# Hash-bucket attention and FFN: queries and keys as scaled high and low float16 halves, hash projections in four column blocks, six kept heads

## The chip, the cores and the metric

The kernel runs on one core of one Trainium2 chip. The metric is device time in microseconds. A core has a matrix engine (TensorE, in the profile PE, with its weight loads as PEld), VectorE (DVE), ScalarE (ACT), GpSimd (POOL), and SyncE (SP), whose queue issues most transfers here. Each engine takes its instructions in the order in which they are written.

## What is computed

The first stage is attention in which a query sees only keys of its own hash bucket; the second is a feed-forward net (FFN) over all tokens. There are 4 batches, 8 heads, 768 positions, 64 numbers per head, 6 hash bits, and an inner FFN width of 2048.

```python
q_bits = (np.einsum('bhsd,dk->bhsk', q, proj) > 0)
k_bits = (np.einsum('bhsd,dk->bhsk', k, proj) > 0)
mask = q_bucket[:, :, :, None] == k_bucket[:, :, None, :]
scores = scale * np.matmul(q, k.transpose(0, 1, 3, 2))
scores = np.where(mask, scores, -1000000000.0)
attn = softmax(scores)                    # with 1e-9 added to the sum
x = (attn @ v), heads side by side        # 3072 x 512
h = x @ w_in
out = (0.5 * h * (1 + erf(h / sqrt(2)))) @ w_out
```

## The kernel before

**Passes.** Attention works head by head. The first batch goes in two passes, one over the first 256 queries and one over the other 512, so that FFN work exists early; the other three batches go in one pass each. A pass prepares the operands of each head (`head`, L608) and then does units of 128 queries against all 768 keys (`unit`, L702): 2 units per head in the first pass, 4 in the second, 6 later, 192 in all. Each pair of heads ends in the product with V (`values`, L822). When all eight heads of a pass are through, its chunks of 256 tokens go through the FFN (L1025 and L1097).

**A head's operands.** `head` loads q and k, transposed and stacked to 128 rows (q in the upper 64, k in the lower), rounds them to fp32r into the tile Aq (the high half), and makes four tiles out of it: Ak gets a copy of the rounded k (L659), Bq and Bk get the other copies (L657, L658) and the low halves, which are what the rounding left (L660, L661). Copies can run on ACT, DVE, POOL or as a transfer on SP's queue; low halves on DVE or POOL. Then q and k are projected on the hash directions, in two column ranges of 256 and 512, each with three fp32r matmuls (L673, L675, L678); ACT takes the sign of each range (L681); two more operations write the mask rows (L691, L695). These rows lower a score by 2^34 for each hash bit in which query and key differ, so that softmax drops all keys of other buckets.

**Which heads are made again.** There are five operand sets in the first pass, of which two live only there. Heads 5 to 7 are made with all query columns and kept for the second pass, which goes through the heads in reverse; the other five are made again, for 512 query columns. Later batches have two sets.

**A unit.** Four fp32r matmuls of 384 columns (L716, L717) make the scores in PSUM; DVE takes the row maximum (L720), checks it (L724) and scales it (L729); ACT does the exponential with its sum (L732); DVE inverts the sum (L742). In the first 40 units TensorE turns the result (L789); in the others it is split into float16 halves (L380 or L377, and L748) and a transfer turns it.

**The order.** Nothing runs in program order. Each operation is a step with a cost, a key, the steps it needs and the buffer ring that it takes; many have a choice of engines. `Plan.order` (L91) plays all steps through on its own clock and gives, whenever an engine is free, the ready step of lowest key to it. The keys come from the unit's number and the offsets in `PAR` (L33); FFN matmuls have keys from 1000 on, so that they take TensorE when no attention step is ready. What comes out is the fixed order of each engine's instructions.

## Time and profile before

The median of three runs is 938.91 us (937.64 to 939.74). The profiled execution has a span of 936.0 us from its first to its last instruction; no other time of that one execution is given, and the 2.9 us to the median are what lies around the span.

| view | PE | DVE | ACT | POOL |
|---|---|---|---|---|
| busy, us of 936.0 | 882.8 | 727.8 | 611.0 | 300.4 |
| busy, 0 to 250 us (100 + 150) | 207.1 | 224.5 | 185.9 | 127.3 |
| busy, 250 to 750 us | 493.3 | 451.7 | 372.1 | 172.2 |
| busy, 750 to 936 us | 182.4 | 51.6 | 53.0 | 0.9 |

A line of the groups reads: source line, engine, operation, what it writes <- what it reads, shapes, count | busy us in all, mean ns of one | idle us of the engine just before them, and what ended it. In a line of the timeline the first number is the start and the second the length in us; a bracket gives the idle time before it. In a line of the chain of waits the numbers are start and length of a piece of the chain that ended last. A line of the windows gives the stretch, its length, then the busy time of each engine asked for, with instruction counts, the granted clock of TensorE, the share of DMA and GB/s. PE's matmuls are pipelined, so that one starts long before the last has ended.

### The profile page before, as it was taken

The page shows a single profiled execution, that of the slowest core. Times are in us where ns is not written, and L with a number is a line of the kernel's source. Part 1 is how long each engine was busy: PE and PEld are TensorE (multiplying, and loading weights), DVE is VectorE, ACT ScalarE, POOL GpSimd, SP SyncE. Part 2 cuts the span into 40 slices and gives each one's busy share as a digit, 9 for nine tenths or more (in the row PEclk, how much of TensorE's full clock was granted, in tenths as well). Part 3 has the DMA queues.
Part 4 walks back from the last instruction along what each step waited for, and adds up shares of the span by engine and source line. Part 5 has one row for each costly group of instructions (what it writes and reads, how often), then busy time and mean ns, then how long its engine had stood idle before and what let it go on. Part 6 is the DMA issues. An engine that isn't in the chain of part 4 may idle for free.

```text
span 936.0 us, 17821 instructions
## 1 busy us (share of the span) xinstructions
PE 882.8 (94%) x6728; PEld 645.9 (69%) x6728; DVE 727.8 (78%) x1616; ACT 611.0 (65%) x976; POOL 300.4 (32%) x254
## 2 busy tenths in 40 slices
PE   4788999877999999999999999999999999999998
PEld 3666788756676766677767776766776767676764
DVE  7899989889989899988889999889889972212122
ACT  5676877979676886867876767866788752222221
POOL 3553654556433233533142423342533100000000
PEclk9889999999999999999999999999999999999999
DMA  9447255267777799877797989688885860000000
GB/s 261 147 151 212 71 152 146 65 173 151 161 136 167 144 189 184 171 143 151 145 176 143 201 153 203 125 167 170 150 158 106 151 106 24 1 23 23 1 23 23
DMA packets 300822, 122.81 MB, mean 131 GB/s; under 512 B 241344, under 2 KB 285504, under 8 KB 300736
## 3 DMA queue, kind: packets, MB, share of 16 engines
q1 hardware_dynamic: 300560, 121.67, 60.0%
q8 instruction: 53, 0.87, 0.4%
q14 instruction: 33, 0.27, 0.1%
q10 hardware_dynamic: 176, 0.00, 0.0%
HBM read 45.49 MB, written 6.29 MB: 55 GB/s over the span
## 4 chain that ended last, share of the span: by engine, by line
PE 60%; DVE 8%; DMA 3%; ACT 3%; issue 1%; POOL 0%; SPq 0%; POOLq 0%; ACTq 0%; DVEq 0%
PE hp L1025 22%; PE hp L1097 21%; PE hp L846 6%; PE s L716 5%; PE s L717 4%; DVE rows L720 2%; DVE hl L748 2%; DMA pt<-hl 1%; DMA pt<-wraw 1%; ACT p L732 1%; DVE wraw L748 1%; DVE g L1073 1%; PE hp L673 1%; PE hp L678 1%; PE hp L675 1%
## 5 line engine op out<-in xcount | busy, mean ns | idle before, releaser
L1025 PE MATMUL hp<-x,Win 128*128 128x256 f16 x2304 | 267.0, 273 | 1.2 <-DVE rows L724 1.2
L1097 PE MATMUL hp<-Wout,g 128*128 128x512 f16 x1152 | 261.6, 379 | 0.0
L1025 PEld LDWEIGHTS <-Win 128*128 128x128 f16 x2304 | 219.8, 98 | 41.8 <-issue 13.5
L1097 PEld LDWEIGHTS <-g 128*128 128x128 f16 x1152 | 108.7, 98 | 128.3 <-issue 9.2
L720 DVE TENSOR_REDUCE rows<-s 128x1 f32<-128x768 f32 x192 | 179.3, 949 | 14.1 <-PE s L717 13.4
L732 ACT ACTIVATE p<-s,rows 128x768 f32<-128x768 f32 x143 | 141.1, 987 | 42.5 <-DVE rows L729 27.3
L716 PE MATMUL s<-Ak,Aq 128*128 128x384 f32 x352 | 137.7, 391 | 12.6 <-ACT p L732 7.0
L1035 ACT ACTIVATE h<-hp,ffs 128x512 f32<-128x512 f32 x96 | 65.6, 683 | 119.8 <-PE hp L1025 117.1
L717 PE MATMUL s<-Bk,Bq 128*128 128x384 f32 x352 | 120.5, 342 | 0.0
L380 DVE TENSOR_SCALAR g<-h,ffs 128x512 f16<-128x512 f32 x39 | 21.0, 541 | 112.7 <-ACT h L1059 82.0
L716 PEld LDWEIGHTS s<-Ak,Aq 128*128 128x128 f32 x352 | 67.8, 193 | 34.6 <-ACT p L732 10.9
L846 PE MATMUL hp<-pt,vhl 128*64 128x256 f16 x1368 | 82.3, 274 | 0.8 <-DMA pt<-hl 0.8
L846 PEld LDWEIGHTS <-vhl 128*64 128x64 f16 x1368 | 71.7, 110 | 12.3 <-issue 11.9
L748 DVE SCALAR_TENSOR_TENSOR hl<-p,rows,hl 128x768 f16<-128x768 f32 x72 | 76.0, 1058 | 2.8 <-ACT hl L377 1.6
L1073 DVE SCALAR_TENSOR_TENSOR g<-h,ffs,g 128x512 f16<-128x512 f32 x96 | 76.0, 810 | 2.4
L789 PE MATMUL hp<-dr,p 128*128 128x128 f32 x480 | 67.0, 296 | 8.2 <-DVE pt L380 2.4
L789 PEld LDWEIGHTS hp<-dr,p 128*128 128x128 f32 x480 | 63.2, 208 | 13.5 <-POOL dr L380 3.2
L717 PEld LDWEIGHTS s<-Bk,Bq 128*128 128x128 f32 x352 | 68.1, 193 | 1.2
L732 ACT ACTIVATE wraw<-s,rows 128x768 f32<-128x768 f32 x49 | 48.3, 986 | 13.8 <-DVE rows L729 5.7
L681 ACT ACTIVATE sign<-hp,off 44x256 f32<-44x256 f32 (+1 forms) x74 | 41.5, 570 | 22.7 <-PE hp L678 22.0
L400 POOL TENSOR_TENSOR Bq<-raw,Aq 64x768 fp32r<-64x768 f32 (+1 forms) x23 | 40.9, 1776 | 23.4 <-ACT Aq L377 13.0
L380 POOL TENSOR_SCALAR hl<-p,rows 128x768 f16<-128x768 f32 x24 | 26.3, 1097 | 63.1 <-DMA pt<-hl 42.0
(154 smaller groups left out, 1256.4 us busy)
## 6 DMA issues: line engine op xcount, KB each, us to landing
raw<-qk SPq DMA_DIRECT2D x29, 384.0 KB, 3.5
vraw<-v SPq DMA_DIRECT2D x25, 384.0 KB, 4.2
wraw<-w_in SPq DMA_DIRECT2D x16, 512.0 KB, 4.4
wraw<-w_out SPq DMA_DIRECT2D x16, 512.0 KB, 4.8
out<-o SPq DMA_DIRECT2D x11, 512.0 KB, 2.9
Ak<-Aq SPq DMA_DIRECT2D x19, 192.0 KB, 3.3
rawe<-qk SPq DMA_DIRECT2D x8, 384.0 KB, 3.1
Bk<-Aq SPq DMA_DIRECT2D x16, 192.0 KB, 3.3
```

What stands on the lines that cost most here:

```text
L380: on.tensor_scalar(out=out, in0=in_, scalar1=scale, scalar2=bias, op0=ALU.mult, op1=ALU.add)
L716: nc.tensor.matmul(to, aq[:, qs], ak[:, n], start=True, stop=False)
L717: nc.tensor.matmul(to, bq[:, qs.start - q0 : qs.stop - q0], bk[:, n], start=False, stop=True)
L720: nc.vector.tensor_reduce(out=nm, in_=both(sp), axis=AX.XY, op=ALU.max, negate=True)
L732: nc.scalar.activation(out=buf(ex).rearrange("p (b k) -> p b k", b=2), in_=both(sp), func=AF.Exp, scale=sc, bias=nb, accum_out=ssum,)
L748: nc.vector.scalar_tensor_tensor(out=buf(hi)[:, 1], in0=buf(ex), scalar=r, in1=buf(hi)[:, 0], op0=ALU.mult, op1=ALU.subtract,)
L789: nc.tensor.matmul(buf(step[0])[:, (k - k0) * P : (k - k0 + 1) * P], buf(ex)[:, words(k)], buf(dg), start=True, stop=True,)
L846: nc.tensor.matmul(pv[j * D : (j + 1) * D], buf(vh)[:, tv, kt, j * D : (j + 1) * D], buf(holds[j][0])[:, tp * KT + kt, :nt], start=kt == 0 ...
L1025: nc.tensor.matmul(buf(pair[0])[:, j * ch[1] : (j + 1) * ch[1]], win_hl[:, f0 // WB1, tw, pr, f0 % WB1 : f0 % WB1 + P], x[:, tx, pr, : ch[1]],
L1035: nc.scalar.activation(out=bufs["h"][0][:, 2 * fp : 2 * fp + 2, :nt], in_=buf(pair[0])[:, : 2 * nt].rearrange("p (j k) -> p j k", j=2), fu ...
L1073: nc.vector.scalar_tensor_tensor(out=gt[:, 1, s2, :nt], in0=h[:, s2, :nt], scalar=sg, in1=gt[:, 0, s2, :nt], op0=ALU.mult, op1=ALU.subtract,)
L1097: nc.tensor.matmul(buf(banks[u]).rearrange("p (c f) -> p c f", c=NWB), gt[:, tg, f, u * P : (u + 1) * P], wout_hl[:, :, tw, ft], start=ft ...
```

## The change

- All four operand tiles are float16. So that float16 suffices, each head gets a scale: DVE takes the largest magnitude in each row of the loaded head, two one-column matmuls against blocks of ones (`twin`) sum these over q's and k's rows, and four one-column DVE operations make a power of two out of it (`head_scale`). The rounding multiplies by it; the low half is scaled input less high half, one operation on DVE or two on POOL. The unit's check multiplies by the inverse (`back`) instead of a constant.
- The hash directions are float16 halves too. Columns 0 to 383 and 384 to 767 of q and of k are projected as four blocks of 32 array columns, with two terms: eight matmuls of 384 columns. One ACT operation takes all signs, and four operations write mask rows, each 24 rows by 384 columns. The sign's offsets come in by eight small transfers on SP's queue (`set_up`).
- With half the bytes, eight sets fit in the first pass, six stay for the second (heads 0 to 5), which makes heads 6 and 7 again, and four serve later batches. The second pass goes in forward order. The first makes all heads with all query columns.
- There are two buffers each for loaded heads of later passes, of the first pass, and for output (`o`, also used in scaling the weights).
- All keys and engine offsets in `PAR` have new numbers, and some costs in the plan differ. FFN, softmax and the product with V compute as before.

```diff
 NEARLY = 2
-RAWE = 1
-KEEP = 3
+RAWE = 2
...
+OB = 2
...
-BIG = 2.0**34
+PAR = dict(
+    SU=-208.01, NM_DVE=-120.92, NM_ACT=-21.45, NM_Pool=27.77, NM_SP=-123.06, NL_DVE=-286.91, NL_Pool=-152.59,
...
+    EV_ACT=-157.8, EV_DVE=400.19, EV_Pool=-118.56, GH_ACT=204.98, GH_DVE=104.62, GH_Pool=-464.69, NS0=-62.77,
+    NS1=-38.83, NS2=-129.58,
+)
+FULL = 65504.0
+FAR = 2.0**30
...
-        "s": 2, "hp": 4, "p": 2, "hl": 2, "raw": 1, "rawe": RAWE, "sign": 1, "dr": 2, "pt": NTH + 1,
-        "x": NTH, "vraw": 1, "vhl": 2, "wraw": 3, "o": 1, "diag": 1, "h": 1,
+        "s": 2, "hp": 4, "p": 2, "hl": 2, "raw": 2, "rawe": RAWE, "sign": 1, "dr": 2, "pt": NTH + 1,
+        "x": NTH, "vraw": 1, "vhl": 2, "wraw": 3, "o": OB, "diag": 1, "h": 1,
     }
-    NSET = 2
+    NSET = 4
+    NKEEP = 6
...
-        "sign": ring(const, "sign", [2 * 32, S], F32, 1),
+        "sign": ring(const, "sign", [P, S // 2], F16, 1),
...
-        "raw": ring(const, "raw", [P, S], F32, 1),
+        "raw": ring(const, "raw", [P, S], F32, rings["raw"]),
...
-    sets = [
-        [const.tile([P, S], F32R, tag=f"{nm}{i}", name=f"{nm}{i}") for nm in ("Aq", "Ak", "Bq", "Bk")]
-        for i in range(NSET)
-    ]
+    names = ("Aq", "Ak", "Bq", "Bk")
+    sets = [[const.tile([P, S], F16, tag=f"{nm}{i}", name=f"{nm}{i}") for nm in names] for i in range(NSET)]
...
-    rest = const.tile([P, S], F32R, tag="rest", name="rest")
-    x_ops = [t[:, :S] for t in ring(const, "x", [P, NPAIR * TC], F32R, NTH, NTH)]
-    sets.append([x_ops[0], x_ops[1], rest, x_ops[2]])
+    rest = const.tile([P, 2, S], F16, tag="rest", name="rest")
+    x_ops = [t[:, : 2 * S].rearrange("p (k n) -> p k n", k=2) for t in ring(const, "x", [P, 2 * NPAIR * TC], F16, NTH, NTH)]
+    for a, c in ((x_ops[0], x_ops[1]), (x_ops[2], rest)):
+        sets.append([a[:, 0], a[:, 1], c[:, 0], c[:, 1]])
...
+    for i in range(NKEEP, NKEEP + NEARLY):
+        sets.append([early.tile([P, S], F16, tag=f"{nm}{i}", name=f"{nm}{i}") for nm in names])
...
-    hash_hi = const.tile([P, KR + HR], F32R, tag="hash_hi", name="hash_hi")
-    hash_lo = const.tile([P, HR], F32R, tag="hash_lo", name="hash_lo")
...
+    twin = const.tile([P, 2, P], BF16, tag="twin", name="twin")
+    hash16 = const.tile([P, 2, 32], F16, tag="hash16", name="hash16")
+    off16 = const.tile([P, 1], F32, tag="off16", name="off16")
+    tops = const.tile([P, B * H + 3], BF16, tag="tops", name="tops")
+    hs = const.tile([P, B * H + 3, 8], F32, tag="hs", name="hs")
...
-    cleared = {}
-        def clear(ak=ak, box=box):
-            on = nc.vector if box[0].engine == "DVE" else nc.gpsimd
-            on.memset(ak[D:].bitcast(F32), 0.0)
-
...
+    def set_up():
+
+        top, w = tops[:, :1], hs[:, 0]
+        n_tops[0] += 1
+
+        def sums():
+            on = nc.gpsimd
+            on.memset(twin, 0.0)
+            for n in range(2):
+                rr = slice(n * D, (n + 1) * D)
+                on.memset(twin[rr, 0, rr], 1.0)
+                on.memset(twin[rr, 1, (1 - n) * D : (2 - n) * D], 1.0)
+            on.memset(hash16, 0.0)
+
+        def offsets():
+            for n in range(4):
+                for m in range(2):
+                    r0 = n * 32 + m * 2 * NBIT
+                    nc.sync.dma_start(out=off16[r0 : r0 + 2 * NBIT], in_=offset[: 2 * NBIT])
+
+        def clear():
+            nc.vector.memset(off16, 0.0)
+
+        def largest():
+            nc.vector.tensor_reduce(
+                out=top, in_=praw[:, :NBIT], axis=AX.X, op=ALU.max, apply_absolute_value=True
+            )
+
+        key = PAR["SU"]
+        a = add("Pool", 1.4, sums, key, [])
+        z = add("DVE", 0.1, clear, key, [])
+        o = add("SP", 0.5, offsets, key, [z])
+        m = add("DVE", 0.1, largest, key, [])
+        sc = head_scale(top, w, key, [a, m], 1)
+
+        def wide(n):
+            return hash16[:, n, : 4 * NBIT].rearrange("p (m i) -> p m i", m=2)
+
+        def high():
+            for m in range(2):
+                nc.vector.tensor_scalar(
+                    out=wide(0)[:, m], in0=praw, scalar1=w[:, 4:5], scalar2=None, op0=ALU.mult
+                )
+
+        def low():
+            for m in range(2):
+                nc.vector.scalar_tensor_tensor(
+                    out=wide(1)[:, m], in0=praw, scalar=w[:, 4:5], in1=wide(0)[:, m],
+                    op0=ALU.mult, op1=ALU.subtract,
+                )
+
+        hi = add("DVE", 0.2, high, key, [sc])
+        return [add("DVE", 0.2, low, key, [hi]), o]
+
+    def head_scale(top, w, key, needs, n):
+        def total():
+            for k in range(n):
+                nc.tensor.matmul(buf(pm)[:, k : k + 1], twin[:, k], top, start=True, stop=True)
+
+        def exponent():
+            nc.vector.tensor_scalar(
+                out=w[:, :n].bitcast(I32), in0=buf(pm)[:, :n].bitcast(I32), scalar1=0x7F800000,
+                scalar2=None, op0=ALU.bitwise_and,
+            )
+
+        def inverse():
+            nc.vector.tensor_scalar(
+                out=w[:, 2 : 2 + n], in0=w[:, :n], scalar1=2.0 if n > 1 else 2.0**-100, scalar2=2.0**-12,
+                op0=ALU.max, op1=ALU.mult,
+            )
+
+        def scale():
+            nc.vector.reciprocal(out=w[:, 4:5], in_=w[:, 2:3])
+
+        def back():
+            nc.vector.tensor_scalar(
+                out=w[:, 5:6], in0=w[:, 2:3], scalar1=w[:, 3:4], scalar2=SCALE, op0=ALU.mult, op1=ALU.mult
+            )
+
+        pm = add("PE", 0.06 + 0.08 * n, total, key, needs, takes="hp")
+        e = add("DVE", 0.12, exponent, key, [pm])
+        free(pm, [e])
+        e = add("DVE", 0.07, inverse, key, [e])
+        if n > 1:
+            e = add("DVE", 0.07, back, key, [e])
+        return add("DVE", 0.07, scale, key, [e])
+
+    def head(b, h, i, key, clear, cl):
+
+        n = n_tops[0]
+        n_tops[0] += 1
+        top, w = tops[:, n : n + 1], hs[:, n]
+        sc = w[:, 4:5]
+        aq, ak, bq, bk = sets[i]
+        upper, lower = slice(0, D), slice(D, P)
+
+        def load():
+            nc.sync.dma_start(out=buf(raw), in_=qk[b, h])
+
+        def largest():
+            nc.vector.tensor_reduce(
+                out=top, in_=buf(raw), axis=AX.X, op=ALU.max, apply_absolute_value=True
+            )
+
+        def high():
+            affine(hi.engine, aq, buf(raw), sc)
+
+        def add_move(dst, src, rd, rs):
+            box = []
+
+            def move():
+                out, in_ = sets[i][dst][rd], sets[i][src][rs]
+                if box[0].engine == "SP":
+                    nc.sync.dma_start(out=out, in_=in_)
+                else:
+                    affine(box[0].engine, out, in_)
+
+            on = {
+                "DVE": (0.27, PAR["NM_DVE"]), "ACT": (0.75, PAR["NM_ACT"]), "Pool": (0.9, PAR["NM_Pool"]),
+                "SP": (0.45, PAR["NM_SP"]),
+            }
+            box.append(add(on, 0, move, key + PAR[f"DUP{cl}"], [hi], port=True))
+            return box[0]
+
+        def add_low(dst, rd, rs):
+            box = []
+
+            def low():
+                out, a = sets[i][dst][rd], aq[rs]
+                x = buf(raw)[rs]
+                if box[0].engine == "DVE":
+                    nc.vector.scalar_tensor_tensor(
+                        out=out, in0=x, scalar=sc[rs], in1=a, op0=ALU.mult, op1=ALU.subtract
+                    )
+                else:
+                    affine("Pool", x, x, sc[rs])
+                    subtract("Pool", out, x, a)
+
+            on = {"DVE": (0.94, PAR["NL_DVE"]), "Pool": (2.8, PAR["NL_Pool"])}
+            box.append(add(on, 0, low, key + PAR[f"LOW{cl}"], [hi], port=True))
+            return box[0]
+
+        raw = add("SP", 1.43, load, key - PAR["HQ"], takes="raw" if cl else "rawe")
+        mx = add("DVE", 0.87, largest, key + PAR[f"NS{cl}"], [raw])
+        sc_ = head_scale(top, w, key + PAR[f"NS{cl}"], [mx, set16[0]], 2)
+        hi = add(affine_on("RND", S, True), 0, high, key, [sc_, *clear], port=True)
+        m1 = add_move(2, 0, upper, upper)
+        m2 = add_move(3, 0, lower, lower)
+        m3 = add_move(1, 0, upper, lower)
+        lq = add_low(2, lower, upper)
+        lk = add_low(3, upper, lower)
+        free(raw, [lq, lk])
+
+        space = add("none", 0, lambda: None, key, [m1, m2, lq, lk], takes="sign")
+        HS = S // 2
+
+        def signs_of():
+            return buf(space)
+
+        def project():
+            for t in range(2):
+                for half in range(2):
+                    n = slice(half * HS, (half + 1) * HS)
+                    for k, x in enumerate((bq, bk)):
+                        r0 = half * 64 + k * 32
+                        nc.tensor.matmul(
+                            buf(pp)[r0 : r0 + 32, :HS], hash16[:, t], x[:, n], start=t == 0, stop=t == 1,
+                            tile_position=(0, r0),
+                        )
+
+        def sign():
+            nc.scalar.activation(out=signs_of(), in_=buf(pp)[:, :HS], func=AF.Sign, bias=off16)
+
+        pp = add("PE", 0.45, project, key + PAR[f"PRJ{cl}"], [space, *set16], takes="hp")
+        sg = add("ACT", 0.1 + 0.833e-3 * HS + 0.186, sign, key + PAR[f"PRJ{cl}"], [pp])
+        free(pp, [sg])
+        masks = []
+        rows = slice(D, D + 4 * NBIT)
+        for half in range(2):
+            for k, dst in enumerate((0, 1)):
+                box = []
+
+                def mask(half=half, k=k, dst=dst, box=box):
+                    r0 = half * 64 + k * 32
+                    affine(
+                        box[0].engine, sets[i][dst][rows, half * HS : (half + 1) * HS],
+                        signs_of()[r0 : r0 + 4 * NBIT], FULL / 2, FULL / 2 if k == 0 else -FULL / 2,
+                    )
+
+                on = {
+                    "DVE": (0.18, PAR["NK_DVE"]), "ACT": (0.42, PAR["NK_ACT"]), "Pool": (0.56, PAR["NK_Pool"])
+                }
+                needs = [sg, m2, m3] if k == 0 else [sg]
+                box.append(add(on, 0, mask, key + PAR[f"MSK{cl}"], needs, port=True))
+                masks += box
+        free(space, masks)
+        return [m3, *masks], w[:, 5:6]
...
-    def head(b, h, i, key, clear, qr, cl):
...
-    def unit(t, i, q0, qs, cl, whole, made, place):
-
-        aq, ak, bq, bk = sets[i]
+    def unit(t, i, qs, cl, whole, made, place, back):
+
...
         def scores():
+            aq, ak, bq, bk = sets[i]
+            kk = slice(0, D + 4 * NBIT)
             for half in range(2):
                 n = slice(half * S // 2, (half + 1) * S // 2)
                 to = both(sp)[:, half]
-                nc.tensor.matmul(to, aq[:, qs], ak[:, n], start=True, stop=False)
-                nc.tensor.matmul(to, bq[:, qs.start - q0 : qs.stop - q0], bk[:, n], start=False, stop=True)
+                nc.tensor.matmul(to, aq[kk, qs], ak[kk, n], start=True, stop=False)
+                nc.tensor.matmul(to, bq[:, qs], bk[:, n], start=False, stop=True)
...
-                out=sc, in0=nm, scalar1=BIG / 2, scalar2=SCALE, op0=ALU.is_lt, op1=ALU.mult
+                out=sc, in0=nm, scalar1=FAR, scalar2=back, op0=ALU.is_lt, op1=ALU.mult,
...
-        sp = add("PE", 0.72, scores, t - PAR[f"QK{cl}"], made, takes="s")
+        sp = add("PE", 0.66, scores, t - PAR[f"QK{cl}"], made, takes="s")
...
+    set16 = set_up()
...
-        n_sets = NSET + 1 + NEARLY if n_pass == 0 else NSET + 1 if b == 0 else NSET
+        n_sets = NKEEP + NEARLY if n_pass == 0 else NKEEP if b == 0 else NSET
         n_head = (q1 - q0) // P
         cl = min(n_pass, 1) if b == 0 else 2
-        again = n_pass > 0 and b == 0
-        more = n_pass == 0 and len(FIRST) > 1
-        heads = list(range(2 * NPAIR))[:: -1 if again else 1]
+        heads = list(range(2 * NPAIR))
...
-                cols = (0, S) if more and pos >= len(heads) - KEEP else (q0, q1)
-                made = head(b, h, i, t - lead, last_use.get(i, cleared.get(i, [])), cols, cl)
-                owner[i] = (b, h, cols[0], made)
-            _, _, base, made = owner[i]
+                owner[i] = (b, h, *head(b, h, i, t - lead, last_use.get(i, []), cl))
+            made, back = owner[i][2:]
...
-            if i > NSET:
+            if i >= NKEEP:
...
-                plan.grow("x", k, spare_use)
+                plan.grow("x", k, last_use[NSET + (k - NTH) // 2])
```

126 lines of the change are left out of this document (19 added, 107 removed).

## The prediction

> **What bounds the kernel now.** I read the page's engine totals and its 40 slices first.
>
> ```profile
> PE 882.8 (94%) x6728; PEld 645.9 (69%) x6728; DVE 727.8 (78%) x1616; ACT 611.0 (65%) x976; POOL 300.4 (32%) x254
> PE   4788999877999999999999999999999999999998
> DVE  7899989889989899988889999889889972212122
> ```
>
> TensorE (PE) is full from the fifth slice on, except around slices 8 to 10. VectorE (DVE) is nearly full too, until slice 33, and then almost idle. An average would hide this, so I cut the span where the last product with V ends (778 us), and where the second pass of the first batch ends (about 225 us).
>
> ```profile
> 0.00:225.00 225.00, 184.83 (x1386) 151.07 (x1387) 200.88 (x459) 166.51 (x310) 111.13 (x99) 0.96 0.55 152
> 225.00:778.00 553.00, 543.60 (x4291) 392.38 (x4292) 492.22 (x1103) 404.26 (x621) 189.23 (x156) 1.00 0.79 156
> 778.00:936.00 158.00, 154.41 (x1056) 102.47 (x1052) 34.72 (x55) 40.21 (x46) 0.00 (x0) 1.00 0.04 14
> 0.00:100.00 100.00, 71.11 (x437) 57.68 (x437) 87.55 (x194) 65.12 (x124) 44.98 (x46) 0.91 0.63 186
> ```
>
> The columns after the length are PE, PEld, DVE, ACT, POOL busy. Before 225 us PE idles 40 us, 29 of them in the first 100: there is not yet an FFN to fill it. From 225 to 778 us it idles 9 us of 553, and after that it runs FFN alone. So from 100 us on a microsecond taken off PE is a microsecond off the end, as long as attention itself does not end later. How much later it may end, the chain of waits tells:
>
> ```profile
> 774.60 4.05 PE hp L846 x72
> ...
> 820.43 10.48 PE hp L1025 x96
> ...
> 862.12 10.48 PE hp L1025 x96
> ...
> 914.27 18.14 PE hp L1097 x84
> ```
>
> One FFN chunk of 256 tokens takes 862.12 - 820.43 = 41.7 us. The last batch has three, 125.1 us, and none can start before attention ends at 778.6. PE ends at 914.27 + 18.14 = 932.4, that is 153.8 us after, so 28.7 us of FFN of the batch before is still waiting there. The span cannot be below the attention's end + 125.1 + 3.6 (store).
>
> **The change part by part.** Spacing of matmuls, not their duration, is PE's price, as they are pipelined.
>
> ```profile
> 402.10 0.47 PE L673 MATMUL hp<-Aq,hash_lo 128*44 128x256 f32 x1
> ...
> 403.32 0.34 PE L716 MATMUL s<-Ak,Aq 128*128 128x384 f32 x1
> ...
> 403.85 0.34 PE L717 MATMUL s<-Bk,Bq 128*128 128x384 f32 x1
> ...
> 434.70 6.57 PE hp L1025 x60
> 389.13 5.20 PE hp L1097 x24
> ```
>
> *Scores.* A 384-column matmul of the old type starts every (403.85 - 403.32)/3 = 0.177 us (two lie between). In float16, 256 columns take 6.57/60 = 0.1095 us and 512 take 5.20/24 = 0.2167, so 384 lie at 0.163. Four per unit: 0.708 becomes 0.652 us. After 100 us the groups of the first of each pair are:
>
> ```profile
> L716 PE MATMUL s<-Ak,Aq 128*128 128x384 f32 x328 | 127.4, 389 | 8.6 <-ACT p L732 5.9 <-issue 1.4 <-ACT wraw L732 1.0
> L716 PE MATMUL s<-x,x 128*128 128x384 f32 x20 | 7.4, 370 | 0.0
> ```
>
> Two a unit, so (328 + 20)/2 = 174 units; the other 18 run where PE idles anyway. 174 x 0.056 = 9.7 us saved. Ends: 0 (the old spacing stays) and 174 x 4 x 0.015 = 10.4.
>
> *Projections.* Six matmuls now take 402.10 to 403.32, 1.22 us; the first is noted some 0.19 us early (it starts 0.03 us after the 512-column matmul ahead of it, which needs 0.22), so 1.03 us for a full head. A head of the second pass lacks one of 256 columns: 0.92. After the first pass, near 100 us, come 5 heads of pass two and 8 for each of three batches: 24 x 1.03 + 5 x 0.92 = 29.3 us. New are eight of 384 columns with 32-column weights, four beside each other. The trace has two beside each other, in the product with V:
>
> ```profile
> 640.73 0.34 PE L717 MATMUL s<-Bk,Bq 128*128 128x384 f32 x1
> 641.00 2.15 PE L846 MATMUL hp<-pt,vhl 128*64 128x256 f16 x36
> 643.09 0.43 PE L673 MATMUL hp<-Aq,hash_lo 128*44 128x512 f32 x1
> ```
>
> 36 in 2.09 us is 0.058 each, half of the 0.1095 of a full-width one: they do run side by side. Entering costs 0.27 - 0.18 = 0.09 us, leaving about as much (2.09 - 18 x 0.111). So a head costs 2 x 0.163 + 0.19 = 0.52 us, with 8 x 0.163 + 0.19 = 1.49 as the other end if the four do not overlap. I take 0.52, since the nearest row shows overlap. Two heads instead of five are made in pass two: 26 x 0.52 = 13.5. Saved: 15.8 us; other end, 26 x 1.49 = 38.7, a loss of 9.4.
>
> The Trainium skill (TensorE: Matmul & The Clock Gate, Part 3, "What overlaps and what doesn't") says that weight loads overlap matmuls in flight only where the row group differs, which speaks against column blocks that all use the full rows; the rows at 641.00 disagree for two blocks. The same part gives 2.38 times for three blocks of 32 columns; by that figure eight would cost an estimated 0.55 + 0.19 us, and the sum would be 6 us worse.
>
> *A scale per head.* Each head adds a maximum over 128x768 and four one-column operations on DVE, and two one-column matmuls between them. Their rows:
>
> ```profile
> L720 DVE TENSOR_REDUCE rows<-s 128x1 f32<-128x768 f32 x192 | 179.3, 949 | 14.1 <-PE s L717 13.4
> L724 DVE TENSOR_SCALAR rows<-rows 128x1 f32<-128x1 f32 x192 | 26.8, 146 | 0.9
> L729 DVE TENSOR_SCALAR rows<-rows 128x1 f32<-128x1 f32 x192 | 37.5, 208 | 1.8
> L742 DVE RECIPROCAL rows<-rows 128x1 f32<-128x1 f32 x192 | 31.0, 162 | 7.4 <-ACT rows L377 2.1
> L415 PE MATMUL hp<-diag,ones 128*128 128x128 bf16 x12 | 2.7, 226 | 7.0 <-ACT diag L377 3.9 <-DVE diag L380 1.5 <-POOL diag L380 0.8
> ```
>
> DVE: 0.95 + 0.15 + 0.15 + 0.21 + 0.16 = 1.62 us a head. PE: the nearest row, 128 columns, is 0.226 us for one with its latency, a floor for two is 2 x 0.03 us (the noted start-to-start above); I take 0.15: 26 x 0.15 = 3.9 us lost (ends 1.6 and 11.8). The 7.0 us that PE idled at 12 such matmuls, 0.58 us each, is a wait and not in this; see the rivals.
>
> *Rounding, moves, low halves, signs, masks.* The three moves and both low halves stay, as float16; two sign operations become one; two masks become four shorter ones. All lie on DVE, ACT, POOL and the DMA queue, hidden behind PE after 100 us. DVE's part in the long stretch is the one cover that may go:
>
> ```profile
> 250.00:778.00 528.00, 19.92 (x18) 1.00 0.79 156
> 250.00:778.00 528.00, 56.98 (x34) 1.00 0.79 156
> 350.00:400.00 50.00, 49.15 (x377) 34.11 (x377) 47.95 (x111) 36.45 (x56) 25.11 (x21) 1.00 0.83 173
> ```
>
> (The first two are what reads the raw heads: DVE 18 operations, POOL 34.) DVE then has 492.2 + 24 x 1.62 = 531 us, 96% of 553, the share that it reached at 350 us (47.95 of 50). ACT has 149 us free there and loses a sign operation and moves, so it can take over the "high" halves that DVE makes now. I take it as holding, narrowly: attention ends near 778 us. PE's work after 100 us falls by 9.7 + 15.8 - 3.9 = 21.6 us, less than the 28.7 us of FFN that are left over there, so PE does not run dry.
>
> *Start.* Two chains grow.
>
> ```profile
> 5.59 0.84 ACT L377 ACTIVATE Aq<-rawe 128x768 fp32r<-128x768 f32 x1 [1.87 <-DMA rawe<-qk]
> 11.47 0.69 PE L716 MATMUL s<-Ak,Aq 128*128 128x384 f32 x1 [1.68 <-POOL Ak L380]
> 1.34 1.06 ACTq L328 DMA_DIRECT2D off<-offset  x2
> ```
>
> Head 0 needs 5.9 us from landing to first score; the maximum, a matmul (0.23) and four small operations put about 1.8 us before it, and hops. Eight small transfers for the sign offsets go onto SP's queue, at 0.53 us each 4.2 us, ahead of loads of raw heads and V issued after them (nothing waits for the offsets until the first sign). Against it, moves are of 2 bytes, the zeroing of old operands goes, and pass two prepares two heads instead of five, at about 40 us of idle PE. Pass one, however, now prepares all 768 query columns of every head instead of 256 for five. I take +2 us, ends -12 and +10.
>
> *Six sets kept, two raw buffers, two output buffers, order and assignment by new numbers:* more lead for loads; nothing on PE.
>
> Sum: -9.7 - 15.8 + 3.9 + 2 = -19.6 us on the profiled span: 936.0 to 916.4. The median of the runs (938.91) is 2.9 above that span, for what lies around it: **919 us**.
>
> **The rivals.** The nearest row for a low half on DVE is that of P:
>
> ```profile
> L748 DVE SCALAR_TENSOR_TENSOR hl<-p,rows,hl 128x768 f16<-128x768 f32 x72 | 76.0, 1058 | 2.8 <-ACT hl L377 1.6 <-POOL hl L380 0.9
> ```
>
> (a) *DVE paces attention; slower.* If the low halves move from POOL to DVE (POOL must now do two operations for each), 48 x 1.06 us less the 19.9 that they take now is +31 on top of 531: 562 us, and at 96% the stretch takes 585 instead of 553. Attention ends at 225 + 585 = 810 us, + 128.7 = 939, + 2 from the start, + 2.9: 944. It decides as soon as attention ends after 788, and makes the kernel slower than before from 807. For it: DVE's 9s in the slices; against it: 149 us free on ACT and 364 on POOL.
>
> (b) *PE waits for the scale.* PE takes its work in a written order; a scale matmul that it reaches before DVE's maximum holds all scores and FFN behind it. At 0.58 us (L415) and 34 heads, 20 us: 939, no change. Against it: the maximum depends on a load alone, and four sets in place of two allow it early.
> (c) *Column blocks run one after another:* 25.2 us more, 944. The rule on weight loads quoted above would bring this; the V rows speak against it.
> (d) *The start shortens as well.* If fewer heads in pass two and the second output buffer take away the 14 us that PE idles between 100 and 225 (40.2 - 28.9 = 11.3, and as much again in the first 100 us at most): 919 - 2 - 14 = 903.
>
> **How the numbers follow.** Chances: forecast 0.48, (a) 0.11, (b) 0.14, (c) 0.04, (d) 0.20, else 0.03. A difference under 0.2% (1.9 us) can't be told from none here. Faster: forecast and (d) whole, 0.10 of (b) where the waits are shorter than 0.58 us, 0.04 of the rest: 0.82. Same: 0.05, mostly (b). Slower: 0.13. Range 898 to 939: from a (d) with 5 us more to (b) in full, which leaves out (a), (c) and a deeper (d), 0.2.
>
> **What would show it.** Scores spaced 0.163 us apart; eight projection matmuls within 0.55 us; PE's total near 860; FFN after attention's last V product still over 125 us with attention ending at or before 786 us. Wrong would be: idle before the scale matmuls of over 10 us in sum, eight projection matmuls over 1 us, or attention ending after 800 us with PE idle before it.

## The result

The changed kernel takes 931.16 us (median of 8 runs, 928.18 to 935.01) where the kernel before took 938.21 in the same comparison: a ratio of 0.9923, 95% interval 0.9903 to 0.9942. A second comparison, among the experiments below, gave 929.14 us and a ratio of 0.9871 (0.9843 to 0.9898). So it is faster by about 1% (0.8 to 1.3%); the forecast of 919 us meant 2%. One execution of one kernel below (u1) took 1781.57 us, nearly twice as long as the others, and is left out of its median. The profiled execution took 928.35 us with a span of 926.4.

The page of the changed kernel, its engine totals and the slices of PE and DVE:

```profile
PE 857.1 (93%) x6857; PEld 576.7 (62%) x6857; DVE 734.4 (79%) x1734; ACT 607.8 (66%) x990; POOL 347.1 (37%) x323
PE   1578899996999999999999999999999999999998
DVE  6888999999989999999999999899889961212122
```

PE's total fell from 882.8 to 857.1, near the 860 of the forecast. But the span fell by only 9.6: PE's idle time grew from 53.2 to 69.3 us. To see where, I cut both spans at two row maxima that DVE takes: the 49th, the first of the second batch (called unit 48 below, counted from 0), and the last (unit 191). Before, they start at 220.3 and 755.0 us, after at 223.9 and 743.5. First the windows before (length, then PE, PEld, DVE, ACT, POOL busy, clock, DMA share, GB/s):

```profile
0.00:220.30 220.30, 183.18 (x1358) 149.84 (x1358) 197.10 (x449) 161.85 (x306) 106.64 (x96) 0.96 0.54 152
220.30:755.00 534.70, 522.25 (x4127) 379.48 (x4128) 483.76 (x1091) 399.44 (x612) 193.23 (x159) 1.00 0.80 159
755.00:936.00 181.00, 177.41 (x1245) 116.61 (x1243) 46.97 (x80) 49.69 (x59) 0.49 (x1) 1.00 0.10 25
```

and the same windows after:

```profile
0.00:223.90 223.90, 171.22 (x1364) 122.55 (x1365) 203.48 (x518) 169.61 (x329) 115.84 (x111) 0.93 0.54 153
223.90:743.50 519.60, 506.81 (x4232) 335.62 (x4231) 483.37 (x1138) 387.83 (x602) 230.03 (x212) 1.00 0.79 153
743.50:926.40 182.90, 179.03 (x1264) 118.50 (x1262) 47.59 (x81) 50.40 (x60) 1.25 (x2) 1.00 0.10 26
```

In the long stretch PE has 15.4 us less to do and the stretch is 15.1 us shorter: one for one. In the first 48 units PE has 12.0 us less to do, and yet they end 3.6 us later; PE's idle time there grew from 37.1 to 52.7 us. Behind the last row maximum 1.9 us more went by. That is the whole 9.6: -15.1 + 3.6 + 1.9.

One more cut, at the first row maximum of the second pass (unit 16, at 98.0 us before and 106.8 after), parts the two passes of the first batch. Before, then after:

```profile
0.00:98.00 98.00, 69.61 (x427) 56.49 (x428) 85.55 (x188) 64.44 (x122) 43.15 (x44) 0.91 0.63 188
98.00:220.30 122.30, 113.57 (x933) 93.34 (x932) 111.54 (x262) 97.42 (x185) 63.49 (x53) 1.00 0.47 123
0.00:106.80 106.80, 65.90 (x453) 45.57 (x454) 89.82 (x229) 69.20 (x126) 47.90 (x51) 0.90 0.59 177
106.80:223.90 117.10, 105.32 (x912) 76.97 (x911) 113.66 (x290) 100.40 (x204) 67.94 (x61) 0.96 0.50 131
```

The first pass ends 8.8 us later: PE has 3.7 us less to do in it, but idles 40.9 us in place of 28.4. The second pass takes 5.2 us less. Not all of the PE work missing there is saved, for the new order puts FFN work off. The first matmul of the FFN's first product (L1025 before, L1120 after) starts at 112.6 us before and at 153.3 after. The same windows for these lines alone, before and after (PE busy, count), in the second pass and behind the last row maximum:

```profile
98.00:220.30 122.30, 22.49 (x192) 1.00 0.47 123
106.80:223.90 117.10, 14.71 (x111) 0.96 0.50 131
755.00:936.00 181.00, 77.79 (x696) 1.00 0.10 25
743.50:926.40 182.90, 80.41 (x720) 1.00 0.10 26
```

In the second pass 81 of these matmuls are missing, 8.9 us at the 0.1095 us that one takes in the prediction. They are done later: 24 of them behind the last row maximum, which is most of the 1.9 us there. The granted clock of the second pass also fell, from 1.00 to 0.96; no run here shows what that costs.

The matmuls themselves, in the timeline after (start, length; the PEld line is the loading of the eight projections' weights):

```profile
211.37 0.33 PE L816 MATMUL s<-Ak,Aq 88*128 88x384 f16 x1
211.53 0.33 PE L817 MATMUL s<-Bk,Bq 128*128 128x384 f16 x1
211.79 0.12 PEld L602 LDWEIGHTS <-hash 128*32 128x32 f16 x8 [0.32 <-issue]
211.79 0.34 PE L602 MATMUL hp<-Bq,hash 128*32 128x384 f16 x1
...
211.80 0.34 PE L602 MATMUL hp<-Bk,hash 128*32 128x384 f16 x1
211.96 0.33 PE L602 MATMUL hp<-Bq,hash 128*32 128x384 f16 x1
...
353.72 0.34 PE L602 MATMUL hp<-Bq,hash 128*32 128x384 f16 x1
...
354.16 1.04 PE L1192 MATMUL hp<-Wout,g 128*128 128x512 f16 x4
...
403.67 0.33 PE L816 MATMUL s<-Ak,Aq 88*128 88x384 f16 x1
...
404.83 0.33 PE L817 MATMUL s<-Bk,Bq 128*128 128x384 f16 x1
```

Scores lie 0.165 us apart, as from 403.67 to 404.83 us with six between them (0.163 forecast). Four projections start together, four more 0.17 us later; from the first to the next instruction it is 0.44 us, and entering costs 0.26 - 0.165 = 0.09, so 0.53 us a head (0.52 forecast). And PE's waits (us in total, times, longest):

```profile
PE hp L494 <- DVE tops L537: 25.3, 6, 7.3
PE s L816 <- ACT p L832: 13.1, 18, 2.6
PE s L816 <- ACT wraw L832: 8.2, 12, 1.7
```

PE waited 25.3 us for a head's maximum in front of scale matmuls, which the forecast named as a sign of rival (b). All six of these waits lie before unit 48; behind it no scale matmul waits. The experiments show what this sign is worth.

### The profile page after: what moved, and what is told of

It is laid out like the page before. It is cut to its first block, busy times and chain, and to the rows that moved or that the text cites. A ratio compares the mean times of both kernels' runs of the same rounds, so it can differ in the third digit from the quotient of the medians.

```text
span 926.4 us, 18281 instructions
## 1 busy us (share of the span) xinstructions
PE 857.1 (93%) x6857; PEld 576.7 (62%) x6857; DVE 734.4 (79%) x1734; ACT 607.8 (66%) x990; POOL 347.1 (37%) x323
## 4 chain that ended last, share of the span: by engine, by line
PE 35%; DVE 23%; DMA 4%; issue 4%; ACT 3%; POOL 1%; SPq 0%; POOLq 0%; DVEq 0%; ACTq 0%
PE hp L1192 14%; PE hp L1120 14%; DVE rows L820 5%; DVE hl L848 4%; PE hp L946 3%; DMA pt<-hl 3%; DVE wraw L848 2%; DVE g L1168 2%; PE s L816 2%; PE s L817 2%; DMA pt<-wraw 1%; ACT p L832 1%; DVE rows L824 1%; DVE rows L829 1%; DVE rows L842 1%
## 5 line engine op out<-in xcount | busy, mean ns | idle before, releaser
L1120 PE MATMUL hp<-x,Win 128*128 128x256 f16 x2304 | 269.9, 274 | 0.2
L1120 PEld LDWEIGHTS <-Win 128*128 128x128 f16 x2304 | 223.8, 98 | 41.1 <-issue 5.1
L832 ACT ACTIVATE p<-s,rows 128x768 f32<-128x768 f32 x140 | 138.0, 986 | 45.3 <-DVE rows L829 23.7
L816 PE MATMUL s<-Ak,Aq 88*128 88x384 f16 x360 | 120.9, 336 | 22.8 <-ACT p L832 12.8
L817 PE MATMUL s<-Bk,Bq 128*128 128x384 f16 x360 | 121.1, 336 | 0.0
L386 DVE TENSOR_SCALAR g<-h,ffs 128x512 f16<-128x512 f32 x30 | 15.2, 508 | 107.5 <-ACT h L1154 76.1
L832 ACT ACTIVATE wraw<-s,rows 128x768 f32<-128x768 f32 x52 | 51.3, 987 | 25.5 <-DVE rows L829 15.7
L817 PEld LDWEIGHTS <-Bq 128*128 128x128 f16 x360 | 35.8, 100 | 50.7 <-issue 33.7
L386 POOL TENSOR_SCALAR hl<-p,rows 128x768 f16<-128x768 f32 x34 | 38.2, 1122 | 57.4 <-DMA pt<-hl 34.0
L816 PEld LDWEIGHTS <-Aq 88*128 88x128 f16 x360 | 36.0, 100 | 31.5 <-issue 9.7
L386 POOL TENSOR_SCALAR raw<-raw,hs 64x768 f32<-64x768 f32 x30 | 34.5, 1151 | 43.2 <-ACT Aq L383 35.2
L1154 ACT ACTIVATE h<-h 128x2048 f32<-128x2048 f32 x24 | 45.9, 1911 | 0.4
```

The lines of the kernel that those rows point to most:

```text
L386: on.tensor_scalar(out=out, in0=in_, scalar1=scale, scalar2=bias, op0=ALU.mult, op1=ALU.add)
L816: nc.tensor.matmul(to, aq[kk, qs], ak[kk, n], start=True, stop=False)
L817: nc.tensor.matmul(to, bq[:, qs], bk[:, n], start=False, stop=True)
L832: nc.scalar.activation(out=buf(ex).rearrange("p (b k) -> p b k", b=2), in_=both(sp), func=AF.Exp, scale=sc, bias=nb, accum_out=ssum,)
L1120: nc.tensor.matmul(buf(pair[0])[:, j * ch[1] : (j + 1) * ch[1]], win_hl[:, f0 // WB1, tw, pr, f0 % WB1 : f0 % WB1 + P], x[:, tx, pr, : ch[1]],
```

## The experiments

The forecast's theory is that PE sets the end from 100 us on and that measuring the heads (maximum, scale matmuls, small operations) costs 0.15 us of PE a head and a part of about 2 us at the start, the rest being hidden. Against it stand: measuring costs VectorE's time (A); it costs through the chain behind the maximum (B, and F for the matmuls in it); the late start is handed on (C) or not (D); in the first 48 units VectorE sets the pace and PE's time counts for nothing (G). All edits keep each engine's order except where they move steps; nothing is planned anew. Medians of the kernel before, beside which each ratio stands, were 938.3 us (e1 to e4), 938.0 (e5, e6, s1, q1), 939.2 (c1 to c3, p2), 940.0 (u1, u2, d1) and 941.1 (a2, e8, e9). As the changed kernel itself came out at 0.9923 and at 0.9871, 4.9 us apart, differences of under 5 us between groups are not settled. Gains are given against its 931.16 us where nothing else is said. Each trace is of one execution, which lies up to 6 us beside the median of its runs.

**Leaving the measuring out (e2, e3).**

```diff
+            on.memset(hs[:, 1:, 4:5], 256.0)
+            on.memset(hs[:, 1:, 5:6], 2.0**-19)
...
+        if not measured:          # e2: cl in (0, 1); e3: all heads
+            for step in [mx, *plan.steps[n0:]]:
+                step.emit = lambda: None
```

> The changed kernel with a fixed scale for the ten heads of the first batch: their maxima, scale matmuls and small operations are left out, everything else keeps its place (the part of the computation left out is the measuring of the scale). Theory A: 5 to 7 us earlier first scores (about 17 us), and 923 to 927 us. Rival B: 10 of 34 heads, so a third of what leaving it out in all heads gains.

> The same fixed scale for all 34 heads (measuring left out everywhere). Theory A: like e2 within 2 us, since in later batches the measuring is hidden behind TensorE. Rival B: 24 x 1.6 us of DVE time fewer in the long stretch, attention ends 10 to 30 us earlier than in e2, total 900 to 915.

Measured: 923.03 us (ratio 0.9842, 0.9826 to 0.9857) and 916.68 us (0.9773, 0.9755 to 0.9791). Measuring costs 14.5 us in all, 8.1 for the ten heads of the first batch and 6.4 for the other 24. The 6.4 are between two runs of one comparison; the other two figures rest on the 931.16. With the second comparison's ratio of 0.9871 it is 9.2 us in all (0.9871 - 0.9773, of 938 us), 2.7 of them for the ten heads. Either way it is the largest saving of the study. Without measuring the kernel takes 916.7 us, where the forecast, less its own 5.9 us for the scale (3.9 and the 2 at the start), would be 913. e2 came in theory A's range, but not by its mechanism: the first scores start at 22.8 us, not near 17. e3 came between the two ranges. The windows of e3:

```profile
0.00:219.20 219.20, 168.42 (x1330) 119.98 (x1331) 187.82 (x442) 169.13 (x329) 118.45 (x112) 0.96 0.55 157
219.20:730.70 511.50, 504.98 (x4200) 335.04 (x4199) 466.75 (x1043) 388.20 (x602) 225.43 (x212) 1.00 0.79 155
```

Against the changed kernel the first 48 units are 4.7 us shorter (DVE 15.7 us less busy, PE only 2.8), the long stretch 8.1 us (PE 1.8 less busy, its idle time 12.8 to 6.5). PE's total is 5.1 us lower. So about a third of the price is PE's own time.

**Its halves (e5, e6).** e5 writes no maximum and puts a constant in its place; e6 keeps the maximum and drops what stands behind it.

```diff
+            on.memset(tops[:, 1:], 4.0)        # e5
+        mx.emit = lambda: None
...
+            for step in plan.steps[n0:]:       # e6, with e3's constants
+                step.emit = lambda: None
```

> Left out: the 34 maxima of heads on VectorE (0.95 us each, 32 us in all); a constant stands in their place, and the scale matmuls and the four small operations behind them run on as they are, for all 34 heads. Theory A (VectorE's time for the maxima is what measuring costs): most of the 14.5 us that leaving out all of the measuring gave comes back, so 917 to 921 us. Rival B (the chain behind the maximum costs: scale matmuls for which TensorE waits in order, small operations with their latency): under 4 us comes back, 927 to 931 us.

> Left out: the scale matmuls and the small operations of the 34 heads; the scale is a constant, and the 34 maxima run on VectorE but nobody reads them. Theory A (the maxima's VectorE time is the cost): 926 to 931 us, as the changed kernel. Rival B (the chain behind them is the cost): 916 to 920 us. If the two parts add, this run and the one without maxima share the 14.5 us between them.

Measured: 924.69 us (0.9834, 0.9799 to 0.9869) and 921.43 us (0.9812, 0.978 to 0.9843). Neither theory alone: 6.5 us come back without the maxima, 9.7 without what follows (3.5 and 5.5 by the ratios against 0.9871); the sum is near the whole both times.

**What behind the maximum costs (c1, a2, e8, e9).** c1 makes the scale in one small operation on the path in place of three, e8 drops the matmuls only, e9 the small operations only; a2 is the changed kernel again.

```diff
-                scalar2=None, op0=ALU.bitwise_and,
+                scalar2=0x7F800000, op0=ALU.bitwise_and, op1=ALU.bitwise_xor,      # c1
...
+            for k in range(n if n == 1 else 0):                                    # e8, the matmuls
...
+                in0=(buf(pm)[:, :1] if n == 1 else w[:, 6:8]).bitcast(I32), scalar1=0x7F800000,
...
+            for step in plan.steps[n0 + 1 :]:                                      # e9
+                step.emit = lambda: None
```

> Every head is still measured, by a maximum and a pair of scale matmuls as before, but the scale comes out of one small VectorE operation in place of three (the exponent's bits are masked and inverted in one operation, for which the ones of the summing matrix become 2 to the power -11); the way back out of the scale takes two further ones that the rounding does not wait for, three in all in place of four. Left out: the guard for a head whose entries are all zero. Theory B (the chain behind the maximum is part of the cost: 9.7 us came back when it was left out): a third to a half of it comes back, 3 to 5 us, so 926 to 928 us. Rival F (it is the waiting on TensorE's matmuls, not the count of small operations, that costs): 930 to 932 us.

> The changed kernel itself, as the base for the two runs beside it on the same chip: 930 to 932 us.

> Left out: the 68 one-column scale matmuls. The maxima run and nobody reads them; the four small operations read a constant and run on. Theory F (in the part of measuring behind the maxima it is the matmuls that cost, for which TensorE waits in order and for which the small operations wait): 921 to 924 us, most of the 9.7 us that leaving out matmuls and small operations together gave. Rival B (the small operations' time on VectorE costs): 928 to 932 us.

> Left out: the four small VectorE operations of the 34 heads, the scale being a constant. The maxima and the scale matmuls run, so TensorE still waits in order for each maximum. Theory F: 928 to 932 us, as the changed kernel. Rival B: 921 to 924 us.

Measured: c1 930.80 us (0.9909, 0.9887 to 0.9931), nothing gained. a2 929.14 (0.9871), e8 933.46 (0.9928, 0.9905 to 0.9952), e9 927.34 (0.9858, 0.9834 to 0.9882). e8, without the scale matmuls, is 4.3 us slower than a2, where theory F expected some 8 us less; e9, with them, comes just under F's range. PE idles 932.3 - 858.0 = 74.3 us of the span in e8 (a2: 929.4 - 855.6 = 73.8). But e8 is no clean test: its first small operation reads two columns in SBUF in place of PSUM and is held by POOL (last section), and DVE's total is 748.5 us in place of 735.8. The clean pair is e9 and e6, which differ by the scale matmuls alone: 927.34 and 921.43, so the matmuls cost 5.9 us (4.3 by the ratios). In the two profiles the first 48 units differ by 1.4 us and the long stretch by 6.6 (519.5 and 512.9); there PE has 2.6 us less to do without them and idles 4.0 us less. So theory F is not out. PE's waits in e8 say where the 25.3 us went:

```profile
PE s L817 <- ACT p L833: 21.9, 23, 6.0
PE hp L603 <- DVE Bq L569: 12.3, 2, 11.3
PE s L817 <- ACT wraw L833: 9.2, 10, 1.9
```

The waits are now at the projections and at the scores, and in e6, too, PE waits 10.6 us at one projection and 21.3 at scores. So PE had little else to do at those places before unit 48, and the wait at the scale matmul was for the most part only its first name. e9's 1.8 us lie within the spread: the small operations alone, beside the matmuls, cost nothing that can be told. Of the 9.7 us, then, 4 to 6 are the matmuls' once the small operations are gone; how the rest arises stays open.

**Measuring on ScalarE (q1).** A sum of squares there in place of the maximum.

```diff
-            nc.vector.tensor_reduce(
-                out=top, in_=buf(raw), axis=AX.X, op=ALU.max, apply_absolute_value=True
-            )
+            nc.scalar.activation(out=junk, in_=buf(raw), func=AF.Square, accum_out=top)
```

> Nothing is left out: a head's measure is the sum of its squares, taken on ScalarE with an accumulating Square (an estimate by the exponential of the same size, 0.9 us each) in place of the maximum on VectorE (0.95 us each), at the same places in the order; the exponent is halved by a shift in the small operation that is there already. VectorE's busy time falls by 32 us and ScalarE's grows by some 30. Theory A (VectorE's time for the maxima is the cost): 918 to 924 us. Rival E (ScalarE's exponentials free the score buffers, and 0.9 us more ahead of one of them delays the scores as much): 930 us or more.

Measured: 934.61 us (0.9962, 0.9941 to 0.9983), slower. DVE's total fell to 711.6 us, but ACT's rose to 635.7, and the long stretch grew to 524.9 us. It is in rival E's range: here the same work on ACT is no cheaper.

**The start (s1, e1, e4, c2, c3).** s1 moves the steps that the first scores need 8 us forward, and the loading and measuring of the second pass's heads 8 us back; e1 moves the latter behind the steps planned for 62 us, which gives their scale matmuls other PSUM buffers where needed; e4 loads the sign offsets in one transfer in place of eight; c3 is c1 with e4, c2 is c3 with s1.

```diff
+        first, todo = set(), list(targets)     # s1: all that the first scores need
...
+        return s.start - lead if s in first else s.start + lag if s in later else s.start
...
+    steps = put_later(steps, second, 62.0)     # e1
...
-            for n in range(4):                 # e4
-                for m in range(2):
-                    r0 = n * 32 + m * 2 * NBIT
-                    nc.sync.dma_start(out=off16[r0 : r0 + 2 * NBIT], in_=offset[: 2 * NBIT])
+            nc.sync.dma_start(out=off16, in_=offset)
```

> Nothing is left out. In the order of the work, all that the first scores need (load, measuring, rounding, low halves, projections and signs of head 0) is put 8 us earlier among the steps of the first 40 us, and the loading and measuring of the two heads of the second pass 8 us later. Theory C (the late first score, with the first row maximum at 27.7 us where it was at 13.2, is passed on to the end): the first row maximum comes near 19 us, TensorE's idle time in the first 100 us falls by 7 us or so, and the time is 922 to 925 us. Rival D (the units 0 to 16 are paced by VectorE, whose work is the same): the 16th row maximum stays within 2 us of 106.8 and the time is 929 to 932 us.

> The changed kernel, in which loading and measuring the two heads of the second pass (load, maximum, two matmuls, four small operations each) is issued behind the steps that the plan starts at 62 us instead of ahead of the first head's work; every other step keeps its place. Theory A (the missing gain lies in the start: the order puts work in front of the first scores that is not needed yet): the first score matmul comes 2 to 4 us earlier than 23.8 us, and the end by as much: 927 to 929 us against 931. Rival B (the measuring of heads costs DVE time in the whole attention, the start does not matter because what comes after it catches up): 930 to 932.

> The changed kernel with the sign offsets brought in by one transfer instead of eight (the array is laid out by rows beforehand). SP's queue is free 4 us earlier at 13.8 us, so the V and weight loads behind it land earlier. Theory A: 1 to 4 us earlier, 927 to 930. If those loads are not what the start waits for: 931.

> The kernel with one small operation on the path (guard for an all-zero head left out), and the sign offsets loaded in one transfer in place of eight. If both act and add: 1 to 3 us under the one without the offsets' edit, 924 to 927 us. If the offsets' edit did nothing (its interval overlapped with the changed kernel's): the same as that one within 1 us.

> Both of these edits and the earlier place of the first head (the guard for an all-zero head left out). In the run that moved the first head alone the scores came 5.6 us earlier, but the row maxima kept their place in VectorE's queue and the time did not fall. Theory D (VectorE's queue paces the first units): the same as without the move, within 2 us. Theory C (an early first score pays once the measuring takes less of VectorE): 3 us or more under it, 921 to 923 us.

Measured: s1 930.85 us (0.9897, 0.9858 to 0.9936): the first scores start at 18.2 us in place of 23.8, the first row maximum keeps its place in DVE's queue (28.4 us, 27.7 in the changed kernel), and the median does not move. Its profile is of an execution 5.9 us under its median; there unit 16 comes at 103.1 us, 3.7 earlier than in the changed kernel, but with u2 below, whose first pass is unchanged, it comes at 102.6. e1 941.93 (1.005, 1.003 to 1.0071), 11 us slower than the changed kernel, outside both of its ranges. Its first scores do come 2.6 us earlier (21.2), but unit 16 comes at 112.2 us and unit 48 at 229.6, and the long stretch takes 526.2 us; PE's total is 857.8, 0.7 more than in the changed kernel, so nearly all of it is idle time. Which wait begins it is not known. The same work in a slightly other order can cost nearly as much as all the measuring, so the new order that came with the change is a rival of its own, and no run tests it. e4 928.61 (0.991, 0.9878 to 0.9941) and c3 927.63 (0.9872, 0.9852 to 0.9892): 2.5 and 3.2 us under the kernels without that edit, each time within or near the spread. c2 928.79 (0.9894, 0.9871 to 0.9916): the earlier head adds nothing here either. By the medians theory C falls. None of these versions but e1 stands clear of the changed kernel.

**Whose time counts where (p2, u1, u2, d1).** p2 issues each head's projections twice; u1 (first ten heads) and u2 (the other 24) make them run one after another; d1 takes the maxima of the first ten heads twice.

```diff
-            for t in range(2):
+            for t in (0, 1, 0, 1):                         # p2
...
+                        if cl in (0, 1):                   # u1; u2: cl in (2,)
+                            nc.tensor.matmul(
+                                buf(pp)[:, :HS], hash16[:, t, 96 - r0 : 224 - r0], x[:, n],
+                                start=t == 0 and r0 == 0, stop=t == 1 and r0 == 96,
+                            )
+                            continue
...
+            for _ in range(2 if cl < 2 else 1):            # d1, around the maximum
```

> Every head's eight projection matmuls are issued twice, with the same result; nothing else differs. A set takes 0.44 us between the first start and the last end, so 34 sets more are 15 us of TensorE. If TensorE's time goes to the end one for one, as the forecast took it for what the projections save: 944 to 948 us. Rival: the projections lie in TensorE's idle time (69 us of the span): under 5 us, 931 to 936 us.

> The result is the same. For the ten heads prepared in the first two passes, the eight projection matmuls run one after another: each has 128 columns of weights, 32 of the signs' and zeros, and adds into the same 128 rows. By the spacing of 0.165 us a set takes 1.4 us in place of 0.53, so TensorE gets 8.7 us more work, all in the first 224 us. Theory G (there VectorE and its order set the pace, and TensorE's time is idle time anyway): unit 48 comes within 2 us of 223.9 and the time is 931 to 933 us. Rival (TensorE's time goes to the end one for one everywhere, as the forecast took it from 100 us on): 938 to 941 us.

> The same edit for the 24 heads of the later batches alone: TensorE gets 24 x 0.87 = 21 us more work between 224 and 744 us. Theory G: there TensorE sets the pace (12.8 us idle of 519.7), and the time is 947 to 953 us. Rival (as in the run with the projections twice, less than half of TensorE's time reaches the end): 934 to 941 us.

> The result is the same. The maxima of the ten heads prepared in the first two passes are taken twice, 9.5 us more of VectorE in the first 110 us. Theory G (VectorE paces this stretch): unit 48 comes 5 to 9 us later and the time is 936 to 940 us. Rival (the stretch waits for other things, VectorE has 20 us of idle time in it): under 2 us, 930 to 933 us.

Measured: p2 934.61 us (0.995, 0.9933 to 0.9968), u1 930.44 (0.9884, 0.986 to 0.9908), u2 938.59 (0.9991, 0.9972 to 1.001), d1 934.87 (0.994, 0.9919 to 0.9961). The first two windows of u1:

```profile
0.00:225.80 225.80, 176.10 (x1364) 126.32 (x1365) 206.50 (x518) 169.99 (x329) 115.84 (x111) 0.91 0.53 151
225.80:746.80 521.00, 506.64 (x4233) 335.51 (x4232) 484.13 (x1139) 388.02 (x602) 230.37 (x212) 1.00 0.79 153
```

of u2:

```profile
0.00:221.50 221.50, 169.75 (x1370) 121.35 (x1371) 203.76 (x518) 169.32 (x329) 117.47 (x111) 0.95 0.55 154
221.50:754.10 532.60, 521.28 (x4227) 350.94 (x4226) 489.27 (x1139) 388.50 (x602) 226.94 (x212) 1.00 0.76 149
```

and of d1:

```profile
0.00:231.70 231.70, 172.03 (x1370) 123.52 (x1371) 212.52 (x527) 169.53 (x329) 115.48 (x110) 0.91 0.52 147
231.70:752.90 521.20, 507.66 (x4228) 336.18 (x4226) 483.84 (x1139) 388.16 (x602) 235.17 (x212) 1.00 0.79 153
```

u1 put 4.9 us more PE work into the first 48 units, and they end at 225.8 us (223.9 in the changed kernel's profile, 225.5 in its second one): nothing to be told apart, and the time is no longer. d1 put 9.0 us more DVE work there, and they end at 231.7. u2 put 14.5 us more PE work into the long stretch, and it is 13.0 us longer. So in the traces u2 and d1 speak for theory G: PE's time counts in the long stretch, DVE's in the first one. All of d1's delay is there by unit 16 (114.0 us, 106.8 in the changed kernel), so it is the first pass that it shows. u1's PE work, most of it in the first pass too, can't be told from the spread.

The medians are less clear. Taken against u1 on the same chip, u2 costs 8.1 and d1 4.4 us, a little over half of what the traces show. u2 stayed below G's range, inside that of its rival (934 to 941), and d1 came between its two ranges. One reason is the price: a serial set takes 1.30 us in u2, not 1.4, so it is 0.77 a head and not 0.87, 18 us in all:

```profile
381.20 0.32 PE L603 MATMUL hp<-Bq,hash 128*128 128x384 f16 x1
...
382.50 0.71 PE L1126 MATMUL hp<-x,Win 128*128 128x256 f16 x5
```

The other is the first stretch: u2's first 48 units, whose work is the changed kernel's, ended at 221.5 us in its profile; this stretch varies by some 4 us from run to run. p2 came in its rival's range. Its second sets added 8.9 us to PE's total (866.0) and 3.4 us to the median. Half of them fall in the first stretch, and in p2's profile that ends at 228.1 us, 2.6 to 6.6 later than in the three profiles where it is unchanged. So that PE's time counts for nothing there is not shown; u1 speaks for it, p2 against it.

The first row maxima of the second pass (unit 16) and of the second batch (unit 48) over all profiles, sorted by what DVE is busy before unit 48:

| run | DVE busy before unit 48 | PE busy | unit 16 at | unit 48 at |
|---|---|---|---|---|
| e3, no measuring | 187.8 | 168.4 | 101.8 | 219.2 |
| q1, measuring on ACT | 192.0 | 171.7 | 103.7 | 223.5 |
| e2, ten heads not measured | 192.4 | 169.8 | 101.1 | 219.1 |
| e5, no maxima | 192.8 | 172.0 | 103.7 | 221.4 |
| before | 197.1 | 183.2 | 98.0 | 220.3 |
| e6, maxima only | 198.0 | 170.4 | 104.7 | 222.1 |
| e9, no small operations | 199.3 | 171.8 | 106.6 | 223.5 |
| s1, first head first | 202.2 | 168.5 | 103.1 | 220.2 |
| e1, second pass's heads later | 203.3 | 171.5 | 112.2 | 229.6 |
| c3, one operation, one offset | 203.4 | 172.0 | 105.7 | 223.2 |
| changed kernel | 203.5 | 171.2 | 106.8 | 223.9 |
| c1, one operation on the path | 203.5 | 170.7 | 106.1 | 224.0 |
| c2, c3 with s1 | 203.6 | 170.8 | 105.1 | 223.4 |
| u2, later heads serial | 203.8 | 169.8 | 102.6 | 221.5 |
| a2, changed kernel again | 204.4 | 170.3 | 107.5 | 225.5 |
| e4, one offset transfer | 205.1 | 170.8 | 105.9 | 224.0 |
| u1, serial projections | 206.5 | 176.1 | 108.3 | 225.8 |
| e8, no scale matmuls | 206.7 | 172.3 | 106.9 | 227.5 |
| p2, projections twice | 206.8 | 175.6 | 108.8 | 228.1 |
| d1, maxima twice | 212.5 | 172.0 | 114.0 | 231.7 |

From the first row to the last DVE's work grows by 24.7 us and the time by 12.5. PE's column does not sort it: the kernel before has the most PE work by 7 us and comes fourth by time. From unit 16 to unit 48 all versions of the changed kernel take 117 to 121 us, so most of what they differ by arises in the first pass. There the ten heads' maxima make a series: with none of them measured unit 16 comes at 101.1 and 101.8 us, with the first pass as in the changed kernel at 102.6 to 107.5 (changed kernel, a2, u2), with the maxima taken twice at 114.0.

Three things limit this. Among rows that lie near each other DVE's column does not sort the time: e1 has the changed kernel's work and ends 5.7 us later, u2 2.4 us earlier. DVE's busy time is in part itself an outcome: in u1 and p2 it is 2 to 3 us higher than in the changed kernel and a2 with the same operations. And q1 names a second engine: DVE 192.0, but unit 48 at 223.5, with ACT 12 us busier.

## Why the prediction was right and wrong

In the forecast's own prices, sorted into stretches (144 of its 174 units and 24 of its 26 heads belong to the long one, the others to the second pass):

| stretch | forecast | trace |
|---|---|---|
| first pass (to unit 16) | +2 start | +8.8 |
| second pass (units 16 to 48) | -1.7 scores, -3.6 projections, +0.3 scale = -5.0 | -5.2 |
| units 48 to 191 | -8.1 scores, -12.2 projections, +3.6 scale = -16.7 | -15.1 |
| behind the last maximum | 0 | +1.9 |
| sum | -19.7 | -9.6 |

*Scores and projections: right.* 0.165 and 0.53 us were measured where 0.163 and 0.52 stood; the old score spacing was 0.177. The column blocks do run side by side, and u2's long stretch, where they do not, is 13.0 us longer. Rival (c) is out. (By the rule of the Trainium skill, page "TensorE: Matmul & The Clock Gate", Part 3, "What overlaps and what doesn't", the weight loads of blocks in one row group would not overlap with matmuls in flight; here four matmuls with weights of their own start within 0.01 us, and the weights of the next four are loaded by 211.91 us, while the first four run, so the trace disagrees for column blocks.)

*PE one for one from 100 us on: not contradicted, but in part luck.* PE's total fell by 25.7 us, to 857.1, near the forecast's 860. That the span fell by only 9.6 is idle time, 16.1 us more of it: 12.5 in the first pass, 3.1 in the second, 0.6 behind it. In the long stretch the step held (15.4 us less work, 15.1 us shorter). In the second pass -5.2 stands against -5.0, but 8.9 us of FFN were put off there, which the forecast did not have, so that this agreement is luck.

*The start and the scale per head: the terms that were mis-sized.* The start stood at "+2 us", and the first pass came out at +8.8, 6.8 of the 10 us that are missing. For the measuring there the forecast counted the chain of one head, some 1.8 us, though the maxima and small operations of all ten heads of the first batch are done there; their 1.62 us of DVE a head were held only against the long stretch ("holding, narrowly"), although its row for the first 225 us shows DVE busy for 200.88. Without measuring these heads (e2) unit 16 comes 5.7 us earlier than in the changed kernel's profile, 3.1 behind the kernel before; with the maxima twice (d1) it comes 7.2 later. (Single executions: with the same first pass, u2's comes 4.2 earlier.) In the long stretch, where the scale stood at 24 x 0.15 = 3.6 us, measuring the 24 heads cost 6.4 us (e2 less e3), of which PE's own time explains 1.8 to 3.1 (the long stretch's PE work in e3 and e6). PE's own share itself was near: its total is 4.5 us lower in e6, 5.1 in e3.

In all, measuring cost 14.5 us (9.2 by the second comparison) in place of 5.9. That covers 8.6 of the 12.2 us between the forecast and the median, or 3.3 of the 10.1 to the second median. The rest has no run of its own: FFN work put off, the new order, and the lower granted clock of the second pass are what the traces leave.

*Rivals (a) and (b).* Attention did not get much longer, as (a) had it; it ended at 768.8 us, 9.9 earlier than before. Of (b) the sign came true, 25.3 us of waits at the scale matmuls where it had 20. But they all lie before unit 48, where PE's idle time is 51.7 us without these matmuls (e6) and 52.7 with them, while the matmuls cost 4 to 6 us (e9 to e6), most of it in the long stretch, where none of them waits. So (b) was wrong as it stands, and that the maximum is early enough, as the forecast held against it, is true of the long stretch only.

*The start.* The first scores came at 23.8 us in place of 11.5, far more than the 2 us forecast, but s1, with 5.6 us of that undone, was no faster. Its price is within the first row of the table and is not separated from that of DVE's work there. Rival (d), a shorter start, did not come.

*From span to time.* The forecast added 2.9 us for what lies around the span. The changed kernel's profiled run took 928.35 us, 1.95 over its span, but lies 2.8 under the median of its runs.
